# FFT and MLP kernel: when the pieces of w_out are converted in the first tile of tokens

## The chip, the cores and the metric

The program runs on one core of a Trainium2 chip. The metric is the device time of one execution in microseconds (us), as the median of several runs. The times shown come from one chip job, the profile from one more execution of the same program.

## What is computed

The input `x` has 4 batches of 3072 tokens of width 256. Three stages follow each other: the real part of a two-dimensional FFT, a first MLP, and a second, gated MLP.

```python
X = np.fft.fft(np.fft.fft(x, axis=1), axis=2).real      # attention stand-in
h = X @ w_in                                            # 256 -> 2048
y = np.maximum(0.01 * h, h) @ w_out                     # 2048 -> 256
xk = mu_k * y + (1 - mu_k) * y_prev                     # y_prev: one token earlier
xr = mu_r * y + (1 - mu_r) * y_prev
v = np.maximum(xk @ w_k, 0) ** 2 @ w_v
out = v / (1 + np.exp(-(xr @ w_r)))
```

The weights `w_in`, `w_out`, `w_k`, `w_v` and `w_r` arrive as 64-bit floats. [...]

## The kernel before

The whole order of the work is written out by hand, engine by engine; the kernel runs under a manual schedule. Each engine, and each queue of DMA issues (SyncE, called SP, and GpSimd, called POOL), works through its own instructions strictly in order and waits at an instruction until what it needs is there.

The first MLP works on 24 tiles of 512 tokens of the symmetric half, six per batch pair of sums and differences. A tile is a loop over 16 units `u`; unit `u` is one block of 128 of the 2048 hidden columns. `step(x, nx)` (L680) issues one unit's work: on TensorE three matmuls into `ps` for the unit (`mm_b`, L611), three for the next unit (`mm_a`, L599), and then, for the unit **two steps earlier**, the twelve matmuls with `w_out` (`outmm`, L622): four with `gh` and the high part `uoh`, four with `gh` and the low part `uol`, four with `gl` and `uoh`. So unit `u` meets `w_out` in step `u + 2`. On VectorE a step has `g` (L688), `ev` (L604) and `gl` (L670); on ScalarE two leaky-ReLU passes (L108) and `gh` (L105). `mm_b` of a unit waits until `ev` has read `ps`.

In the first tile alone (batch 0, tile 0) the weights of the first MLP are made ready beside this work, by `boot(u)` (L562), which is called after `step` of unit `u`. `w_in` and `w_out` come in eight pieces of 256 rows or columns. Piece `q` of `w_out` serves the units `2q` and `2q + 1`, so its high and low part are first read in step `2q + 2`. The conversion of one piece of `w_out` (built by `f64_hi_lo`, L170) has these instructions:

- `first`: ScalarE `h` (L130) and `st` (L148); VectorE `h` (L134), `fv` (L140) and `h` again (L143); POOL the product `r<-st,h` (L149). Its parts have names: `head` is ScalarE's `h`, then come `one`, `two` and `three` on VectorE, and `tail` is ScalarE's `st` with POOL's product.
- `four`: ScalarE `uoh` (L162) and POOL the sum `r<-r,fv` (L163).
- `five`: VectorE `uol` (L167), the low part, from POOL's sum and `uoh`.

Before the change `boot` calls `first` of piece `q + 1` at the even unit `2q`, `four` at the odd unit after it, and `five` one unit later. The parts of piece 0 are called one by one: `head0()` after the first tile's Q half has been split (L834), `mid0()` (which is `one`, `two` and `three`) and `tail0()` in `boot(0)`.

POOL has other work in the same stretch. From unit 11 of the first tile the rows of the next batch are folded (`fold_ops`, L203): for each of six groups `g`, SP loads two tiles (`first(g)`, L216 and L217), and `second(g)` issues four **accumulating transfers** from POOL's queue (L221 to L224). L221, L223 and L224 all add into the same tile `pm`, so each of them waits on POOL until the one before it has landed. Group 0 is issued in unit 11, group 1 in unit 13, group 2 in unit 16. `next_tab` (L485) issues the load of a DFT table (L199), also from POOL, 1158 KB each; `tab_d` is issued in unit 12. `fft_src` (L281) in unit 11 reads the tile `pm` for the last time (VectorE `t0Qe`, L290) before SP may load the next batch into it.

```python
def second(g):
    E = pm[:, g, 0]
    G.dma_start(E, xs[b, g, :, 1], accum_op=ALU.add)
    G.dma_start(st[g], xs[b, g, :, 2:4], accum_op=ALU.add)
    G.dma_start(E, xs[b, g, :, 2], accum_op=ALU.add)
    G.dma_start(E, xs[b, g, :, 3], accum_op=ALU.add)
```

Of the kernel before, what the change touches and what calls it, by code (L numbers as in the profile page):

```python
# [78 lines left out]
def fft_mlp_kernel(ctx, tc, xs, x7, x8, x87, tb, tbs, alt, ce, so, mu, w_in, w_out, w_k, w_v, w_r, out):  # L79
# [24 lines left out]
    def act_copy(o, i):  # L104
        A.activation(o, i, ACTF.Copy)  # L105
# [4 lines left out]
    def hi_lo(hi, lo, src):  # L110
        act_copy(hi, src)
        V.tensor_tensor(lo, src, hi.bitcast(F32), op=ALU.subtract)  # L112
# [46 lines left out]
    def split_steps(z, k, f, parts):  # L159
        def four():  # L160
            z["p"] = parts()
            A.activation(z["p"][0], z["f"], ACTF.Copy, scale=2.0 ** -8)  # L162
            G.tensor_tensor(z["r"], z["r"], z["f"], op=ALU.add)  # L163

        def five():
            hi, lo = z["p"]
            V.scalar_tensor_tensor(lo, z["r"], 2.0 ** -8, hi.bitcast(F32), op0=ALU.mult, op1=ALU.subtract)  # L167
        return (*f64_steps(z, k, f), four, five)

    def f64_hi_lo(hi, lo, st, k, f, fp, ft):  # L170
        z = {"st": st, "fp": fp, "ft": ft}
        head, one, two, three, tail, four, five = split_steps(z, k, f, lambda: (hi, lo))

        def mid():
            one()
            two()
            three()

        def first():
            head()  # L180
            mid()
            tail()
        return first, four, five, (head, mid, tail)


    TAB = {k: i for i, k in enumerate(["a", "b", "a2", "b2", "c", "d", "c2", "d2"])}
# [109 lines left out]
    def fft_mm(b, kind, h, ps, stop):  # L296
        t = tabs[KINDS[kind][h]]
        how = dict(skip_group_check=True) if h else {}
        if (b, kind[1]) == (0, "o"):
            terms = [(odd0[h][:, c, 0 if kind[0] == "P" else 1], t[:, c]) for c in range(3)]  # L300
        else:
            hi, lo = srcs.pop((b, kind, h))
            terms = [(w[:, c], t[:, i, c]) for c in range(3) for w, i in ((hi, 0), (hi, 1), (lo, 0))]
        fw = FW[kind[1]]
        for n, (w, x) in enumerate(terms):
            T.matmul(ps[:, :fw], w, x[:, :fw], start=(h == 0 and n == 0), stop=(stop and n == len(terms) - 1), **how)  # L306
# [25 lines left out]
    def first_p(ps, ev):  # L332
        fft_mm(0, "Po", 1, ps, True)
        y = pqp.tile([P, CP], F32, tag="P", bufs=2, name="c0Po")
        classes[0, "P", "o"] = y
        hi = mv.tile([P, W], F32R, tag="Ph", bufs=2, name="Ph0_0")
        lo = mv.tile([P, W], F32R, tag="Pl", bufs=2, name="Pl0_0")
        act_copy(hi[:, :J], ps[:, :J])
        V.scalar_tensor_tensor(y[:, J:2 * J], ev[:, :J], 2.0, ps[:, :J], op0=ALU.mult, op1=ALU.subtract)
        V.tensor_tensor(lo[:, :J], ps[:, :J], hi[:, :J].bitcast(F32), op=ALU.subtract)  # L340
        hi_lo(hi[:, J:], lo[:, J:], y[:, J:W])
        return [hi, lo]

    def first_q(ps, ev):
        fft_mm(0, "Qo", 1, ps, True)
        y = pqp.tile([P, CP], F32, tag="Q", bufs=2, name="c0Qo")
        classes[0, "Q", "o"] = y
        act_copy(y[:, :J], ps[:, :J])
        n = W - J
        V.scalar_tensor_tensor(y[:, J:W], ev[:, :n], -2.0, ps[:, :n], op0=ALU.mult, op1=ALU.add)  # L350
        act_copy(y[0:1, :J], cs0[0:1, :J])
        act_copy(y[0:1, J:W], cs0[0:1, J:W])

        def rest():
            V.scalar_tensor_tensor(y[:, W:2 * J], ev[:, n:J], -2.0, ps[:, n:J], op0=ALU.mult, op1=ALU.add)
            act_copy(y[0:1, W:CW["o"]], cs0[0:1, W:CW["o"]])
        return rest
# [9 lines left out]
    def split_tile(b, t, nm):  # L367
        hi = mv.tile([P, W], F32R, tag=nm + "h", bufs=2, name=f"{nm}h{b}_{t}")
        lo = mv.tile([P, W], F32R, tag=nm + "l", bufs=2, name=f"{nm}l{b}_{t}")
        o = 0  # L370
        for par, at, n in PIECES[t]:
            hi_lo(hi[:, o:o + n], lo[:, o:o + n], classes[b, nm, par][:, at:at + n])
            o += n
        return [hi, lo]
# [14 lines left out]
    win, wout, wps = {}, {}, {}  # L389
# [4 lines left out]
    def w_in_load(q, ahead=False):  # L394
        if q < 8:
            win[q] = load_f64(w_in[:, q * 256:(q + 1) * 256].rearrange("(k p) f -> p k f", p=P), 2, 256, ahead)

    def w_in_parts(q):
        if q < 8:
            win[q] = f64_parts(win[q], 2, 256, F32R)  # L400


    def w_in_mm(q, halves=(0, 1)):
        if q >= 8:
            return
        if halves[0] == 0:
            wps[q] = *win[q], ps_s.tile([P, 512], F32, tag="s", name=f"wps{q}")
        fv, r, ps = wps[q]
        win[q] = ps, slice(q * 256, (q + 1) * 256)
        for i in halves:  # L410
            tabl, tabr = ((cet, cer), (sot, sor))[i]
            o = ps[:, i * 256:(i + 1) * 256]
            for k in range(2):
                T.matmul(o, tabl[:, k], fv[:, k], start=(k == 0), stop=False)  # L414
            for k in range(2):
                T.matmul(o, tabr[:, k], r[:, k], start=False, stop=(k == 1))

    def w_in_split(q):
        if q >= 8:
            return  # L420
        ps, sl = win[q]
        o = ps.rearrange("p (i f) -> p i f", i=2)
        act_copy(wh2[:, :, sl], o)
        V.tensor_tensor(wl2[:, :, sl], o, wh2[:, :, sl].bitcast(F32), op=ALU.subtract)


    def w_in_row(q):
        if q >= 8:
            return
        ps = win.pop(q)[0]  # L430
        for i in range(2):
            f = slice((2 * q + i) * P, (2 * q + i + 1) * P)
            o = ps[:, 2 * i:2 + 2 * i]
            T.matmul(o, woh[:, f], one0, start=True, stop=False)
            T.matmul(o, wol[:, f], one0, start=False, stop=True)
        act_copy(w128[:, 2 * q:2 * q + 2], ps[:, 0:4].rearrange("p (i t) -> p i t", t=2)[:, :, 0])

    def w_out_load(q, ahead=False):
        if q < 8:
            st = load_f64(w_out[q * 256:(q + 1) * 256].rearrange("(k p) d -> p k d", p=P), 2, D, ahead)  # L440
            s = slice(2 * q % HF, 2 * q % HF + 2)
            wout[q] = f64_hi_lo(uoh[2 * q // HF][:, s], uol[2 * q // HF][:, s], st, 2, D, *((mv, "gl") if q < 1 else (stage, "f")))
# [107 lines left out]
        fold_odd(g, x0[g])  # L550
    w_in_parts(2)
    cur = first_p(*po)
    rest_q = first_q(*qo)
    head0, mid0, tail0 = wout[0][3]
    rows.release()
    wo = tc.alloc_tile_pool(name="wo", bufs=1)
    wo.tile([P, 80], F32, name="pad2")
# [4 lines left out]
    def boot(u):  # L562
        q = u // 2
        if u == 0:
            w_in_mm(2, (1,))
            mid0()
            tail0()
            wout[0][1]()
            w_in_load(4)
        elif u % 2 == 0:  # L570
            w_in_row(q + 1)
            w_in_mm(q + 2)
            if 1 < q < 8:
                wout[q][2]()
            if q == 1:
                wout[1][1]()
            if q < 7:
                wout[q + 1][0]()
            w_in_load(q + 4)
        else:  # L580
            if q == 0:
                wout[0][2]()
            w_in_split(q + 2)
            if q == 1:
                wout[1][2]()
            if 0 < q < 7:
                wout[q + 1][1]()
            w_in_parts(q + 3)
            if q == 0:
                wout[1][0]()  # L590
            w_out_load(q + 3)

    def mm_a(x):
# [237 lines left out]
    w_in_mm(2, (0,))  # L831
    ev_a(nx)
    cur += split_tile(0, 0, "Q")
    head0()  # L834
    rest_q()
    for b in range(B):

# [3 lines left out]
        for ti in range(NT):  # L841
# [3 lines left out]
            for u in range(NF):  # L845
# [10 lines left out]
                if b == 0 and ti == 0:  # L856
                    boot(u)
# [27 lines left out]
                if i == qe_u + 1:  # L885
                    if b + 1 < B:
                        first, second, fin, _, load7, sum7, fold7 = fold_ops(b + 1)
# [261 lines left out]
```

## Time and profile before

| what | value |
|---|---|
| median of 3 runs | 1490.97 us (1490.51 to 1491.19) |
| profiled execution, own time | 1490.74 us |
| its span, first to last instruction | 1489.0 us |
| TensorE busy | 1472.1 us (99%) |
| VectorE busy | 1032.1 us (69%) |
| ScalarE busy | 893.5 us (60%) |
| POOL busy | 145.2 us (10%) |
| granted TensorE clock | 1.00 over the span |

The profile divides the span into instructions with a start and a length; an idle time in front of an instruction is printed in square brackets with what ended it. DMA-issuing instructions don't count as busy. Matmuls overlap, so the distance between the starts of two of them says more than their printed length. TensorE is busy nearly all the time, so a look at its few idle times tells where the execution can still become shorter, and at which point another engine could make it longer.

### The profile page before, as it was taken

To read this page: it belongs to the slowest core of one execution; us is meant where nothing else is said; L and a number is where in the kernel's file an instruction comes from. 1 tells how busy PE (TensorE), PEld (TensorE's weight loads), DVE (VectorE), ACT (ScalarE), POOL (GpSimd) and SP (SyncE) were. 2 spreads that over 40 slices of the span, in tenths; PEclk is the share of its full clock that TensorE was granted. 3 is DMA by queue.
4 is the path that set the end of the run, shared out by engine and by line. 5 is a ranking of instruction groups with operands and counts; after the bars stand their busy time and mean duration, and the time that the engine had idled before them with its cause. 6 is when DMAs were issued, how large, how long until landed. Compare 5 with 4: busy or idle time off the path is not lost.

```text
span 1489.0 us, 17784 instructions
## 1 busy us (share of the span) xinstructions
PE 1472.1 (99%) x6520; PEld 1210.1 (81%) x6520; DVE 1032.1 (69%) x1444; ACT 893.5 (60%) x1481; POOL 145.2 (10%) x154
## 2 busy tenths in 40 slices
PE   7999999999999999999999999999999999999998
PEld 4687888888888888888888887888888888888887
DVE  7997667666666766666767666676667666666675
ACT  5566566556566565665666666556565655555554
POOL 2444101131010221010000000000000000000000
PEclk9999999999999999999999999999999999999999
DMA  8657223464032654142320102221212112121200
GB/s 311 179 177 161 53 82 125 173 120 91 15 116 92 193 122 69 36 156 66 105 79 0 57 1 98 72 86 45 83 53 76 64 64 67 61 71 57 72 29 29
DMA packets 86396, 134.24 MB, mean 90 GB/s; under 512 B 29283, under 2 KB 49525, under 8 KB 82724
## 3 DMA queue, kind: packets, MB, share of 16 engines
q1 hardware_dynamic: 70916, 86.49, 17.8%
q0 software_dynamic: 15392, 46.61, 12.5%
q8 instruction: 51, 0.84, 0.2%
q14 instruction: 37, 0.30, 0.1%
HBM read 105.20 MB, written 27.88 MB: 89 GB/s over the span
## 4 chain that ended last, share of the span: by engine, by line
PE 95%; DVE 2%; ACT 1%; DMA 0%; issue 0%; POOL 0%; ACTq 0%; DVEq 0%; POOLq 0%
PE o L622 34%; PE v L989 17%; PE kps L946 17%; PE ps L611 9%; PE ps L599 8%; PE rps L997 4%; PE wps L414 1%; DVE fv L140 1%; PE dps L643 1%; PE cps L461 0%; PE f0Po L306 0%; DVE h L134 0%; PE f0Qo L306 0%; DMA st<-in_w_in 0%; DVE g L688 0%
## 5 line engine op out<-in xcount | busy, mean ns | idle before, releaser
L688 DVE SCALAR_TENSOR_TENSOR g<-ev,ps 128x512 f32<-128x512 f32 x192 | 131.8, 686 | 181.6 <-PE ps L611 181.4
L950 ACT ACTIVATE rl<-kps 128x512 f32<-128x512 f32 x190 | 113.5, 597 | 230.7 <-PE kps L946 227.3
L670 DVE TENSOR_TENSOR gl<-g,gh 128x1024 fp32r<-128x1024 f32 x192 | 239.0, 1245 | 1.4 <-ACT gh L105 1.4
L951 DVE SCALAR_TENSOR_TENSOR k<-kps,rl 128x512 f32<-128x512 f32 x190 | 131.4, 692 | 148.6 <-ACT rl L950 147.7
L105 ACT ACTIVATE gh<-g 128x1024 fp32r<-128x1024 f32 x192 | 202.7, 1056 | 49.3 <-PE o L622 47.6
L622 PE MATMUL o<-gh,uol 128*128 128x512 f32 x768 | 211.3, 389 | 1.1 <-DVE uol L167 1.1
L622 PE MATMUL o<-gh,uoh 128*128 128x512 f32 x768 | 211.3, 389 | 0.0
L622 PE MATMUL o<-gl,uoh 128*128 128x512 f32 x768 | 211.1, 389 | 0.0
L108 ACT ACTIVATE g<-ps 128x512 f32<-128x512 f32 x192 | 114.6, 597 | 157.9 <-DVE g L688 156.7
L622 PEld LDWEIGHTS o<-gh,uol 128*128 128x128 f32 x768 | 144.0, 188 | 31.8 <-DVE uol L167 2.0
L622 PEld LDWEIGHTS o<-gh,uoh 128*128 128x128 f32 x768 | 144.2, 188 | 30.5
L622 PEld LDWEIGHTS o<-gl,uoh 128*128 128x128 f32 x768 | 144.2, 188 | 29.9
L604 DVE SCALAR_TENSOR_TENSOR ev<-cb,w,ps 128x512 f32<-128x512 f32 x192 | 143.3, 746 | 2.2 <-PE ps L599 0.4
L112 DVE TENSOR_TENSOR k2l<-k,k2h 128x512 fp32r<-128x512 f32 x190 | 129.6, 682 | 0.5 <-ACT k2h L105 0.5
L989 PE MATMUL v<-k2h,wvh 128*128 128x512 f32 x382 | 121.6, 389 | 0.1
L989 PE MATMUL v<-k2l,wvh 128*128 128x512 f32 x382 | 121.5, 389 | 0.0
L989 PE MATMUL v<-k2h,wvl 128*128 128x512 f32 x382 | 121.5, 389 | 0.0
L108 ACT ACTIVATE g<-g 128x512 f32<-128x512 f32 x192 | 120.0, 625 | 0.0
L946 PE MATMUL kps<-mh,wkh 128*128 128x512 f32 x380 | 117.3, 390 | 1.5 <-ACT mh L105 0.8
L105 ACT ACTIVATE k2h<-k 128x512 fp32r<-128x512 f32 x190 | 118.4, 623 | 0.0
L946 PE MATMUL kps<-ml,wkh 128*128 128x512 f32 x380 | 117.2, 390 | 0.1
L946 PE MATMUL kps<-mh,wkl 128*128 128x512 f32 x380 | 117.1, 389 | 0.0
(409 smaller groups left out, 2254.9 us busy)
## 6 DMA issues: line engine op xcount, KB each, us to landing
y<-yo SPq DMA_DIRECT2D x24, 512.0 KB
xa<-y SPq DMA_DIRECT2D x24, 512.0 KB
out_dram<-o SPq DMA_DIRECT2D x23, 512.0 KB
tab_a<-in_tbs POOLq DMA_DIRECT2D x8, 1158.0 KB, 6.3
tab_b<-in_tbs POOLq DMA_DIRECT2D x8, 1158.0 KB, 5.5
tab_c<-in_tbs POOLq DMA_DIRECT2D x6, 1158.0 KB, 5.6
tab_d<-in_tbs POOLq DMA_DIRECT2D x6, 1158.0 KB, 5.7
pm<-in_xs POOLq DMA_DIRECT2D x54, 128.0 KB, 3.5
```

Of the source, the lines that this page charges most:

```text
L105: A.activation(o, i, ACTF.Copy)
L108: A.activation(o, i, ACTF.Prelu, alpha=0.01)
L112: V.tensor_tensor(lo, src, hi.bitcast(F32), op=ALU.subtract)
L599: T.matmul(x["ps"], l[:, f], r, start=(i == 0), stop=(i == 2))
L604: V.scalar_tensor_tensor(x["ev"], x["cb"], w128[:, u:u + 1], x["ps"], op0=ALU.mult, op1=ALU.add)
L611: T.matmul(x["ps"], l[:, f], r, start=False, stop=(i == 2), skip_group_check=True)
L622: T.matmul(po[s][h], w[:, u % HF, h * P:(h + 1) * P], g[:, s], start=(u == 0 and i == 0), stop=(u == NF - 1 and i == 2))
L670: V.tensor_tensor(gl, x["g"], x["gh"].bitcast(F32), op=ALU.subtract)
L688: V.scalar_tensor_tensor(g[:, 1], x["ev"], 2.0, x["ps"], op0=ALU.mult, op1=ALU.subtract)
L946: T.matmul(ps, w[:, k, sl], x[:, k], start=(i == 0), stop=(i == 5))
L951: V.scalar_tensor_tensor(k2, ps, 0.0, r, op0=ALU.max, op1=ALU.mult)
L989: T.matmul(vps[m], w[:, f, m * P:(m + 1) * P], x, start=(f == 0 and i == 0), stop=(f == NK - 1 and i == 2))
```

## The change

Nothing is added or removed; instructions trade places on VectorE, ScalarE and POOL. TensorE's and SP's orders stay as they are.

- In `boot`, an even unit `2q` (from 2 on) now calls `first` and `four` of piece `q` (not of piece `q + 1`), and the odd unit `2q + 1` calls `five`, between `w_in_split` and `w_in_parts`. The low part of piece `q` is thus made in unit `2q + 1`, just ahead of step `2q + 2`, which reads it.
- The last piece, 7, is started in unit 14 and finished in unit 15, where it was started in unit 12 and finished in unit 13.
- Of piece 0, `head` and `one` run between P's and Q's last steps of the FFT, `two` after Q's split, and `three` and `tail` in `boot(0)`.

```diff
-        def mid():
-            one()
-            two()
-            three()
-
         def first():
-            head()
-            mid()
-            tail()
-        return first, four, five, (head, mid, tail)
+            for g in (head, one, two, three, tail):
+                g()
+        return first, four, five, (head, one, two, three, tail)
...
     cur = first_p(*po)
+    head0, and0, two0, three0, tail0 = wout[0][3]
     rest_q = first_q(*qo)
-    head0, mid0, tail0 = wout[0][3]
+    head0()
+    and0()
...
         if u == 0:
             w_in_mm(2, (1,))
-            mid0()
+            three0()
             tail0()
             wout[0][1]()
             w_in_load(4)
         elif u % 2 == 0:
             w_in_row(q + 1)
             w_in_mm(q + 2)
-            if 1 < q < 8:
-                wout[q][2]()
-            if q == 1:
-                wout[1][1]()
-            if q < 7:
-                wout[q + 1][0]()
+            if q < 8:
+                wout[q][0]()
+                wout[q][1]()
             w_in_load(q + 4)
         else:
-            if q == 0:
-                wout[0][2]()
             w_in_split(q + 2)
-            if q == 1:
-                wout[1][2]()
-            if 0 < q < 7:
-                wout[q + 1][1]()
+            wout[q][2]()
             w_in_parts(q + 3)
-            if q == 0:
-                wout[1][0]()
             w_out_load(q + 3)
...
     cur += split_tile(0, 0, "Q")
-    head0()
+    two0()
     rest_q()
```

POOL, from the fold of group 0 (unit 11) on, before the change. `r<-st,h` and `r<-r,fv` here are product and sum of piece 7; the `pm` and `xl` rows are the accumulating transfers:

```order
L222 DMA xl_0_1013<-in_xs 128x512
L223 DMA pm_1012<-in_xs 128x256
L224 DMA pm_1012<-in_xs 128x256
L149 TENSOR_TENSOR r<-st,h 128x512
L199 DMA tab_d<-in_tbs 128x2316
L163 TENSOR_TENSOR r<-r,fv 128x512
L221 DMA pm_1012<-in_xs 128x256
L222 DMA xl_1_1016<-in_xs 128x512
L223 DMA pm_1012<-in_xs 128x256
L224 DMA pm_1012<-in_xs 128x256
L221 DMA pm_1012<-in_xs 128x256
L222 DMA xl_2_1126<-in_xs 128x512
```

The same place after it:

```order
L216 DMA xl_0_1002<-in_xs 128x512
L217 DMA pm_1001<-in_xs 128x256
L218 DMA pm_1001<-in_xs 128x256
L149 TENSOR_TENSOR r<-st,h 128x512
L163 TENSOR_TENSOR r<-r,fv 128x512
L193 DMA tab_d<-in_tbs 128x2316
L215 DMA pm_1001<-in_xs 128x256
L216 DMA xl_1_1005<-in_xs 128x512
L217 DMA pm_1001<-in_xs 128x256
L218 DMA pm_1001<-in_xs 128x256
L149 TENSOR_TENSOR r<-st,h 128x512
L163 TENSOR_TENSOR r<-r,fv 128x512
```

The first pair is now piece 6's, with the table's load behind both; piece 7's pair stands behind all four transfers of group 1.

VectorE in unit 11, where the tile `pm` is read for the last time, before:

```order
L604 SCALAR_TENSOR_TENSOR ev<-cb_0_245,w_86,ps 128x512
L670 TENSOR_TENSOR gl<-g,gh 128x1024
L424 TENSOR_TENSOR wl_111<-wps_940,wh_110 128x2x256
L290 TENSOR_TENSOR t0Qe_1006<-pm_125 128x384
L112 TENSOR_TENSOR sl0Qe_1008<-t0Qe_1006,sh0Qe_1007 128x384
```

and after:

```order
L590 SCALAR_TENSOR_TENSOR ev<-cb_0_245,w_86,ps 128x512
L656 TENSOR_TENSOR gl<-g,gh 128x1024
L418 TENSOR_TENSOR wl_111<-wps_929,wh_110 128x2x256
L167 SCALAR_TENSOR_TENSOR uol_323<-r,uoh_322 128x512
L284 TENSOR_TENSOR t0Qe_995<-pm_125 128x384
L112 TENSOR_TENSOR sl0Qe_997<-t0Qe_995,sh0Qe_996 128x384
```

The low part of piece 5 now stands ahead of that read.

VectorE at the start of the first tile, before (`ev` is that of units 0, 1 and 2 in turn, `h` and `fv` are of piece 0):

```order
L350 SCALAR_TENSOR_TENSOR c0Qo<-fe0Qo,f0Qo 128x128
L604 SCALAR_TENSOR_TENSOR ev<-cb_0_245,w_86,ps 128x512
L112 TENSOR_TENSOR Ql_0_343<-c0Qo,Qh_0_342 128x512
L355 SCALAR_TENSOR_TENSOR c0Qo<-fe0Qo,f0Qo 128x256
L688 SCALAR_TENSOR_TENSOR g<-ev,ps 128x512
L604 SCALAR_TENSOR_TENSOR ev<-cb_0_245,w_86,ps 128x512
L134 TENSOR_SCALAR h<-h 128x512
L140 SCALAR_TENSOR_TENSOR fv<-st,h 128x512
L143 TENSOR_SCALAR h<-fv 128x512
```

and after:

```order
L344 SCALAR_TENSOR_TENSOR c0Qo<-fe0Qo,f0Qo 128x128
L134 TENSOR_SCALAR h<-h 128x512
L590 SCALAR_TENSOR_TENSOR ev<-cb_0_245,w_86,ps 128x512
L112 TENSOR_TENSOR Ql_0_346<-c0Qo,Qh_0_345 128x512
L140 SCALAR_TENSOR_TENSOR fv<-st,h 128x512
L349 SCALAR_TENSOR_TENSOR c0Qo<-fe0Qo,f0Qo 128x256
L674 SCALAR_TENSOR_TENSOR g<-ev,ps 128x512
L590 SCALAR_TENSOR_TENSOR ev<-cb_0_245,w_86,ps 128x512
L143 TENSOR_SCALAR h<-fv 128x512
```

The first step of piece 0 stands ahead of unit 0's `ev`, the second behind Q's split, the third behind unit 1's `ev`. On ScalarE piece 0's `h` (L130) likewise moves from behind `Qh` to ahead of it.

## Rows read from the trace of the kernel before

**Rows 1.** The page: busy time, share and instructions of each engine.

```profile
PE 1472.1 (99%) x6520; PEld 1210.1 (81%) x6520; DVE 1032.1 (69%) x1444; ACT 893.5 (60%) x1481; POOL 145.2 (10%) x154
```

**Rows 2.** Busy time by stretch (PE, PEld, DVE, ACT, POOL), granted clock, DMA share, GB/s.

```profile
28.00:60.00 32.00, 28.05 (x129) 20.41 (x128) 29.16 (x41) 21.04 (x39) 15.96 (x12) 1.00 0.92 263
60.00:84.00 24.00, 23.42 (x109) 18.69 (x108) 20.71 (x29) 14.38 (x26) 8.48 (x7) 1.00 0.38 127
84.00:130.00 46.00, 46.00 (x218) 38.25 (x217) 41.12 (x61) 31.68 (x57) 21.87 (x21) 1.00 0.59 167
130.00:1489.00 1359.00, 1353.50 (x6001) 1120.28 (x5999) 920.12 (x1264) 815.53 (x1339) 93.24 (x107) 1.00 0.27 78
```

**Rows 3.** TensorE's waits, whole span: us in total, times, longest us.

```profile
PE ps L611 <- DVE ev L604: 2.2, 3, 1.1
PE o L622 <- DVE uol L167: 1.1, 2, 0.7
...
PE wps L414 <- ACT g L108: 0.3, 1, 0.3
```

**Rows 4.** Timeline of PE: start us, length us, what, [idle before <-releaser].

```profile
34.83 0.50 PE L611 MATMUL ps<-Qh,wh 128*128 128x512 f32 x1 [1.14 <-DVE ev L604]
...
38.10 1.20 PE L622 MATMUL o<-gh,uol 128*128 128x512 f32 x4 [0.71 <-DVE uol L167]
```

**Rows 5.** Timeline of ACT and DVE around the first unit.

```profile
28.32 0.75 DVE L604 SCALAR_TENSOR_TENSOR ev<-cb,w,ps 128x512 f32<-128x512 f32 x1 [0.40 <-PE ps L599]
...
28.93 0.66 ACT L130 ACTIVATE h<-st 128x512 f32<-128x512 f32 x1
...
31.92 0.42 DVE L134 TENSOR_SCALAR h<-h 128x512 uint32<-128x512 uint32 x1
```

**Rows 6.** Timeline of POOL, units 11 to 13: fold of groups 0 and 1.

```profile
115.98 0.85 POOL L224 DMA_DIRECT2D pm<-in_xs  x1 [2.73 <-DVE g L688]
116.54 1.63 POOL L149 TENSOR_TENSOR r<-st,h 128x512 f32<-128x512 f32 x1
117.80 0.90 POOL L199 DMA_DIRECT2D tab_d<-in_tbs  x1
118.41 2.01 POOL L163 TENSOR_TENSOR r<-r,fv 128x512 f32<-128x512 f32 x1
120.36 0.85 POOL L221 DMA_DIRECT2D pm<-in_xs  x1
...
125.08 0.85 POOL L223 DMA_DIRECT2D pm<-in_xs  x1 [2.98 <-DMA pm<-in_xs]
128.33 0.85 POOL L224 DMA_DIRECT2D pm<-in_xs  x1 [2.40 <-DMA pm<-in_xs]
```

**Rows 7.** Timeline of DVE, units 11 to 13: piece 7 and the last read of `pm`.

```profile
104.20 1.05 DVE L290 TENSOR_TENSOR t0Qe<-pm 128x384 f32<-128x384 f32 x1
...
110.64 0.48 DVE L143 TENSOR_SCALAR h<-fv 128x512 uint32<-128x512 uint32 x1
...
120.45 0.69 DVE L167 SCALAR_TENSOR_TENSOR uol<-r,uoh 128x512 fp32r<-128x512 f32 x1 [1.19 <-POOL r L163]
```

**Rows 8.** Timeline of PE: low part's matmuls of units 12 and 14.

```profile
116.53 1.07 PE L622 MATMUL o<-gh,uol 128*128 128x512 f32 x4
...
125.80 1.07 PE L622 MATMUL o<-gh,uol 128*128 128x512 f32 x4
```

**Rows 9.** DMA issues, 109 to 130 us: KB each, median us from issue to landing.

```profile
tab_d<-in_tbs POOLq DMA_DIRECT2D x1, 1158.0 KB, 6.0
```

**Rows 10.** Timeline of POOL: a product and a sum with no VectorE work in their way.

```profile
33.78 1.29 POOL L149 TENSOR_TENSOR r<-st,h 128x512 f32<-128x512 f32 x1 [6.43 <-ACT uoh L162]
...
62.84 1.31 POOL L163 TENSOR_TENSOR r<-r,fv 128x512 f32<-128x512 f32 x1
```

**Rows 11.** Timeline of PE: same four matmuls after its first wait, and later.

```profile
6.54 2.07 PE L414 MATMUL wps<-fv,cet 128*128 128x256 f32 x4 [6.54 <-DVE fv L140]
...
11.22 1.15 PE L414 MATMUL wps<-fv,cet 128*128 128x256 f32 x4
```

## Prediction

> **What bounds the kernel now.** The page comes first: TensorE is busy 99% of the span, every other engine 69% or less [rows 1]. So the execution gets shorter only where TensorE stands idle, and any new wait of TensorE lengthens it. The table by stretch says where it stands: between 28 and 84 us it is busy 28.05 of 32 and 23.42 of 24 us, that is 4.5 us idle; from 84 to 130 us it is busy 46.00 of 46.00, and over the other 1359 us it lacks 5.5 [rows 2]. The list of TensorE's waits names the causes in the first stretch: three waits for `ev` (2.2 us), two for a low part `uol` (1.1), one for ScalarE's `g` (0.3) [rows 3]. In that stretch VectorE is busy 29.16 of 32 us [rows 2]; it is the bound there, and what is queued on it early is what TensorE waits for. Past 84 us the reader should see the reverse: TensorE has no idle time left, so a low part that comes late there is a loss in full.
>
> **The change, first part: units 0 to 6.** Two edits work against each other.
>
> Taken away from VectorE's and ScalarE's early queue is one piece's conversion; from unit 1 on one piece fewer has been converted at any moment, and the odd units no longer carry two conversions. I take the waits for `ev` other than the longest as gone (2.2 less the 1.14 at 34.83 us), the second `uol` wait (1.1 less the 0.71 at 38.10 us) and the 0.3 for `g` [rows 3, 4]: 1.1 + 0.4 + 0.3 = 1.8 us. A group of four matmuls that follows a wait takes 1.20 us [rows 4], one that doesn't 1.07 [rows 8], so four waits fewer return another 0.13 each, 0.5 in all. Gain 2.3 us. The wait at 34.83 I leave, since of unit 1's neighbours only one step of piece 0 moves out and one moves in, and the one at 38.10 too, since piece 0's product and sum still follow `three` and `tail` in unit 0.
>
> Added is a delay of the first unit: ScalarE's `h` (0.66) and VectorE's `h` (0.42) of piece 0 now stand ahead of `Qh` and of unit 0's `ev` [rows 5]. Between 0.4 (VectorE's alone) and 1.1 us (both in a row) of that reaches TensorE; `ev` was idle for 0.40 us in front [rows 5], which takes some of the sum, so 0.8.
>
> Net of this part: 2.3 - 0.8 = **1.5 us gained**. Bounds: all of the 4.5 us of idle time goes (3.7 gained), or nothing does (1.1 lost). ScalarE's moved steps cost nothing further, it is idle a third of the time in both stretches [rows 2]; that idle time hides them, and without it `gh` would come later. SP's order stays; the transfers of later pieces wait in their buffers longer, which nobody waits for.
>
> **The change, second part: pieces 6 and 7 behind the fold.** Here the diff's quiet side is. Piece 6 was started in unit 10, ahead of the fold of group 0; now it starts in unit 12, behind it on POOL. Piece 7 moves from unit 12 to unit 14, behind the fold of group 1. POOL waits at L223 and at L224 until the transfer before has landed, and everything queued behind waits along. The trace shows that this is no fine point: piece 7's product had its last input from VectorE at 110.64 + 0.48 = 111.1 us [rows 7] and started only at 116.54, 0.56 us behind L224 [rows 6]. It did no harm, because unit 14's low part was not read before 125.80 us [rows 8] and was made at 120.45 [rows 7]. Now piece 6 takes that very place, and it is due when unit 12 meets it, at 116.53 us [rows 8].
>
> All times below are on the old clock; the fold starts from `t0Qe` of unit 11, which VectorE reaches earlier by the gain of the first part, so that gain shifts everything alike and is subtracted at the end.
>
> - *Start.* Piece 5's `uol` (0.69) now stands ahead of `t0Qe` [rows 7], which must end before SP may reload `pm`. `t0Qe` took 1.05 us beside POOL's sum there and could be shorter; between 0 and 0.7, I take 0.3. The product of piece 6 starts at 116.54 + 0.3 = 116.8.
> - *Piece 6.* Product and sum take 1.29 and 1.31 us with nothing in their way [rows 10], and VectorE sits waiting, so nothing is; with 0.1 between them POOL is done at 119.5. `uol` takes 0.69 more: 120.2, where 116.53 was wanted. **TensorE waits 3.7 us in step 14.**
> - *Table.* `tab_d` was issued at 117.80 between product and sum [rows 6]; now behind both, at 119.5. It lands 6.0 us after issue [rows 9]: 125.5 where it was 123.8.
> - *Group 1.* Its first transfer, L221, was issued at 120.36 and the next that needs it at 125.08 [rows 6], 4.7 us later, where L223 to L224 is 3.25 (125.08 to 128.33). I read that as L221 standing behind the table in POOL's one queue: L223 came 1.3 us after the table's landing. So L223 now goes at 126.8, L224 at 130.0.
> - *Piece 7.* Product 0.56 us behind L224, at 130.6; with the sum done at 133.3; `uol` at 134.0. Due 125.80 [rows 8]: **8.2 us late**, of which 3.7 are already spent in step 14. With 0.13 for the restart, 8.3.
>
> Behind that `uol` VectorE has `g` and `ev` of the next unit to do (0.75 for `ev` [rows 5]), while TensorE still has eight matmuls with `w_out`; no further wait follows. The fold's later groups come later by as much, and what they make is read in unit 37, over twenty units on, so that costs nothing.
>
> Bounds: if product and sum are stretched as in the old trace (1.63 and 2.01, [rows 6]), each pair takes 1.0 more: 10.3 late. If the table does not hold up group 1, L221 goes at 120.1, L223 at 123.4, L224 at 126.6, `uol` is there at 130.6: 4.9 late.
>
> **Sum.** 8.3 - 1.5 = 6.8 us on top of the profiled execution's own 1490.74: 1497.5 us. The median of the runs lies 0.23 above that execution, so I forecast **1497.8 us**, 0.46% slower.
>
> **Rivals.**
>
> *The low parts are there in time.* The price is the first part alone: 1491.0 - 1.5 = 1489.5, at the best bound 1487.3. The place is POOL between 104 and 117 us: it decides if the way from `t0Qe` to piece 6's `uol` is 3.7 us shorter than I work out, and that to piece 7's 8.2 us. Against it stands the old trace, in which POOL's product waited out the transfers for 5.4 us with its inputs ready [rows 6, 7]; for it only that the new order's transfers are in no row yet. Chance 0.08, a quarter of it below 1488.0.
>
> *The table is not in the way.* Then 4.9 - 1.5 = 3.4: 1494.4. For it speaks that I infer the queueing from a single 4.7 against 3.25. Chance 0.15.
>
> *TensorE comes back slowly from a pause.* After its 6.54 us of waiting at the start the same four matmuls took 2.07 us, and from 11.22 us on 1.15 [rows 11]: twice the time, as at 1.2 in place of 2.4 GHz, although the granted clock is printed as 1.00 in all stretches shown [rows 2]. The slow stretch runs from 6.54 to 11.22, 4.7 us, of which half is lost: 2.3. The pauses of the forecast are 3.7 us in step 14 and 8.2 - 3.7 = 4.5 in step 16; a slow return from the first is swallowed by the second, whose end POOL sets, so one such loss counts: 1500.1. The longest pause after the start was 1.14 us [rows 4], so the trace can't tell what 4 us do. Chance 0.2. The Trainium skill (TensorE: Matmul & The Clock Gate, "Part 1: The HAM clock gate") says that half rate is the state after an idle spell and that only sustained work lifts it; by that rule the sum would be 1500.1, without it 1497.8. The trace agrees with it at the start, and no row here shows it later.
>
> **How the numbers follow.** The forecast has 0.57, with its own range of 1495.5 to 1499.8. To hold 8 in 10 the range goes from **1494.2** (just under the case without the table) to **1501.0** (the slow return, or stretched pairs with little gained early). A measurement of this kernel tells about 0.2% from no change, 3 us. Slower by more than that, above 1494.0: forecast, slow return and two thirds of the table's case, 0.87. Within it: the rest of that case and most of the first rival, 0.11. Faster: 0.02.
>
> **What the changed profile would show.** Two new waits of TensorE, `o L622` for `uol L167`, of some 4 and 4.5 us, in the place where the old table has 46.00 of 46.00; VectorE's two `uol` there idle behind POOL's sum; piece 7's sum on POOL near 132 us; TensorE some 1 to 2 us ahead of the old trace at unit 10. If those two waits are missing, or under 2 us each, the second part is wrong; if the waits for `ev` and the second `uol` still stand before 60 us, the first is. If matmuls behind the long waits run at double their length, the slow return holds.

## The result, and the profile after

The changed kernel takes 1501.7 us (median of 6 runs, 1500.45 to 1502.34), the kernel before, run beside it, 1490.91 (6 runs). The ratio is 1.0071, 95% interval 1.0058 to 1.0084: 10.8 us slower, where 6.8 were forecast. The range ended at 1501.0 and did not hold the time. The sign and the place were right, the size 4 us short. The profiled execution took 1500.71 us, span 1498.9; its span is 9.9 us longer than that of the profile before (1489.0), and its own time lies 1.0 below the median of its runs. The sums below explain the 9.9.

The table by stretch, in the columns of [rows 2]:

```profile
28.00:60.00 32.00, 29.78 (x141) 22.46 (x140) 25.04 (x39) 20.30 (x37) 16.69 (x13) 1.00 0.89 259
60.00:84.00 24.00, 24.00 (x118) 20.13 (x117) 22.49 (x34) 16.34 (x29) 7.27 (x6) 1.00 0.36 116
84.00:130.00 46.00, 40.97 (x177) 32.94 (x175) 32.34 (x51) 27.68 (x49) 18.64 (x17) 0.93 0.60 166
130.00:1498.90 1368.90, 1359.58 (x6019) 1124.56 (x6018) 924.57 (x1270) 818.31 (x1343) 97.14 (x110) 1.00 0.27 78
```

The first two stretches gained, as they were meant to: VectorE is busy 25.04 us where it was 29.16, and TensorE has no idle time left from 60 to 84 us. The third lost 5.0 us of TensorE, and its granted clock is 0.93 on the mean. TensorE's waits (us in total, times, longest), which answer to [rows 3]:

```profile
PE o L608 <- DVE uol L167: 9.5, 3, 5.0
...
PE ps L597 <- DVE ev L590: 1.7, 2, 0.8
```

The waits for `uol` grew from 1.1 to 9.5 us (of each piece of the 64-bit `w_out` the kernel makes two single-precision tensors, the high part `uoh` and the low part `uol`). Where the waits stand shows TensorE's timeline, which answers to [rows 8] (start, length, what, idle before and its releaser); the rows with `Qh,wh` are the first matmuls of units 14 and 17:

```profile
110.27 0.50 PE L597 MATMUL ps<-Qh,wh 128*128 128x512 f32 x1
...
111.76 1.09 PE L608 MATMUL o<-gh,uoh 128*128 128x512 f32 x4
117.89 2.08 PE L608 MATMUL o<-gh,uol 128*128 128x512 f32 x4 [5.03 <-DVE uol L167]
...
124.43 1.09 PE L608 MATMUL o<-gh,uoh 128*128 128x512 f32 x4
...
129.04 1.07 PE L608 MATMUL o<-gh,uoh 128*128 128x512 f32 x4
134.00 2.00 PE L608 MATMUL o<-gh,uol 128*128 128x512 f32 x4 [3.89 <-DVE uol L167]
...
137.98 0.40 PE L597 MATMUL ps<-Qh,wh 128*128 128x512 f32 x1
```

The same two first matmuls in the kernel before:

```profile
114.26 0.39 PE L611 MATMUL ps<-Qh,wh 128*128 128x512 f32 x1
...
128.08 0.39 PE L611 MATMUL ps<-Qh,wh 128*128 128x512 f32 x1
```

So TensorE reaches unit 14 earlier by 114.26 - 110.27 = 4.0 us, and unit 17 later by 137.98 - 128.08 = 9.9. In between lie four losses, 13.9 us together. The four matmuls with `uol` would have started 0.91 us behind the 111.76 and the 129.04 (the distance of such groups in an unhindered step); they start 5.2 and 4.1 us late. And after each wait TensorE runs slowly for a while: from 117.89 to the next step's group with `uoh`, 124.43, are 6.54 us, where the same work took 3.67 in the kernel before (116.53 to 120.20); from 134.00 to unit 17 are 3.98 us, where it took 2.28 (125.80 to 128.08). That is 2.9 and 1.7 us, and 5.2 + 4.1 + 2.9 + 1.7 = 13.9. The table by stretch gives the granted clock (the third column from the right):

```profile
120.00:122.00 2.00, 2.00 (x6) 1.10 (x6) 1.93 (x4) 1.34 (x3) 0.00 (x0) 0.50 0.98 320
...
124.00:126.00 2.00, 2.00 (x10) 1.64 (x9) 1.90 (x4) 1.82 (x3) 0.00 (x0) 1.00 0.88 154
...
134.00:136.00 2.00, 2.00 (x5) 1.62 (x6) 1.89 (x3) 1.11 (x2) 0.91 (x2) 0.53 0.52 76
...
138.00:140.00 2.00, 2.00 (x10) 1.65 (x9) 1.01 (x2) 1.77 (x3) 0.00 (x0) 1.00 0.85 178
```

It is 0.50, the lower of the two levels, or close to it (0.53, where a stretch holds a little of both) for some time behind each wait, and 1.00 in the stretches from 84 to 116 us, ahead of the first wait, and again from 124 and from 138 us.

POOL's timeline answers to [rows 6]:

```profile
113.60 0.85 POOL L218 DMA_DIRECT2D pm<-in_xs  x1 [2.40 <-DMA pm<-in_xs]
114.16 1.60 POOL L149 TENSOR_TENSOR r<-st,h 128x512 f32<-128x512 f32 x1
115.85 1.26 POOL L163 TENSOR_TENSOR r<-r,fv 128x512 f32<-128x512 f32 x1
117.05 0.59 POOL L193 DMA_DIRECT2D tab_d<-in_tbs  x1
117.64 0.89 POOL L215 DMA_DIRECT2D pm<-in_xs  x1
...
126.45 0.86 POOL L217 DMA_DIRECT2D pm<-in_xs  x1 [7.04 <-DMA pm<-in_xs]
129.71 0.86 POOL L218 DMA_DIRECT2D pm<-in_xs  x1 [2.40 <-DMA pm<-in_xs]
130.27 1.61 POOL L149 TENSOR_TENSOR r<-st,h 128x512 f32<-128x512 f32 x1
131.96 1.26 POOL L163 TENSOR_TENSOR r<-r,fv 128x512 f32<-128x512 f32 x1
```

and VectorE's to [rows 7]:

```profile
101.39 0.55 DVE L284 TENSOR_TENSOR t0Qe<-pm 128x384 f32<-128x384 f32 x1
...
117.14 0.69 DVE L167 SCALAR_TENSOR_TENSOR uol<-r,uoh 128x512 fp32r<-128x512 f32 x1 [5.80 <-POOL r L163]
...
133.25 0.69 DVE L167 SCALAR_TENSOR_TENSOR uol<-r,uoh 128x512 fp32r<-128x512 f32 x1 [6.43 <-POOL r L163]
```

Piece 6's product and sum (114.16, 115.85) stand behind L218 of group 0, piece 7's (130.27, 131.96) behind L218 of group 1, and VectorE sits idle for 5.80 and 6.43 us until POOL's sum lets it make `uol`. Between them POOL waits 7.04 us for the transfer that L215 issued, right behind `tab_d`.

### The profile page after: what moved, and what is told of

Read it like the earlier page. It is cut to its first block, busy times and chain, and to the rows that moved or that the text cites. A ratio compares the mean times of both kernels' runs of the same rounds, so it can differ in the third digit from the quotient of the medians.

```text
span 1498.9 us, 17784 instructions
## 1 busy us (share of the span) xinstructions
PE 1475.7 (98%) x6520; PEld 1212.7 (81%) x6520; DVE 1025.5 (68%) x1444; ACT 893.8 (60%) x1481; POOL 145.4 (10%) x154
## 4 chain that ended last, share of the span: by engine, by line
PE 90%; DVE 1%; DMA 1%; POOL 1%; issue 0%; ACT 0%; POOLq 0%; ACTq 0%; DVEq 0%
PE o L608 32%; PE v L975 17%; PE kps L932 17%; PE ps L597 8%; PE ps L585 8%; PE rps L983 4%; DMA pm<-in_xs 1%; PE dps L629 0%; POOL r L163 0%; POOL r L149 0%; PE f1Qe L300 0%; PE f2Qe L300 0%; DMA y<-yo 0%; PE f3Qe L300 0%; PE f3Pe L300 0%
```

## The experiments

All times are medians, with the ratio to the kernel before (1490.8 to 1490.9 in each comparison) and its interval. Diffs are against the changed kernel, except where another is named. "Unit 17" is the start of that unit's first matmul with `Qh,wh`.

### Which part: the spread of piece 0, or pieces 6 and 7

`late_only` puts piece 0's steps back where they were:

```diff
     rest_q = first_q(*qo)
-    head0()
-    and0()
...
             w_in_mm(2, (1,))
+            and0()
+            two0()
             three0()
...
-    two0()
+    head0()
     rest_q()
```

> The changed kernel with piece 0's steps back where they were (all of its VectorE steps in unit 0). Theory (the early gain comes from the pieces moved later; the spread of piece 0's steps only costs 0.8 us at the first unit): TensorE's 0.8 us wait ahead of its first Q matmul goes, units 3 to 12 are as early as in the changed kernel or up to 0.8 us earlier, and since POOL's fold sets the end of both waits the total stays within 1 us of the changed kernel's 1501.7. Rival (the spread brings part of the gain): unit 14 starts 1 to 2 us later than in the changed kernel (111 to 112 us), the total is 1502 to 1503.

1500.99 us, ratio 1.0069 (1.0054 to 1.0084). Unit 14 comes at 110.30 and unit 17 at 138.52: early gain and late loss are both there. The wait of 0.81 us in front of the first unit, which the spread of piece 0 costs, is gone here, but two later waits are longer (1.12 for 0.84 us, 0.71 for 0.53), and unit 3 starts at 42.87 where the changed kernel has 42.86. In the total the spread is worth less than this comparison can tell.

`early67` leaves the change to pieces 0 to 5. It starts piece 6 in unit 11, on POOL ahead of the fold of group 0, and piece 7 in unit 12, behind group 0 but ahead of the table and of group 1:

```diff
-            if q < 8:
+            if q < 6:
                 wout[q][0]()
                 wout[q][1]()
+            if q == 6:
+                wout[6][2]()
+                wout[7][0]()
+                wout[7][1]()
             w_in_load(q + 4)
...
-            wout[q][2]()
+            if q != 6:
+                wout[q][2]()
+            if q == 5:
+                wout[6][0]()
+                wout[6][1]()
             w_in_parts(q + 3)
```

> The changed kernel, but pieces 6 and 7 keep places ahead of or right at the first fold group: piece 6 is started in unit 11 ahead of the fold of group 0 on POOL, and piece 7 in unit 12, ahead of the table. Theory (the loss is the two sums that queue behind accumulating transfers, and the slow clock that these waits bring): both waits of TensorE for a low part after 84 us go, no stretch runs at a granted clock below 1.00, and the early gain of 4.0 us that the changed kernel shows at unit 14 (110.27 against 114.26 us) stays to the end: about 1487.0 us, 1486.3 to 1488.3. Rival (the early gain is only borrowed, later waits take it back whatever the place of pieces 6 and 7): 1490 to 1491.

1491.01 us, ratio 0.9998 (0.9989 to 1.0008). No wait for `uol` is left in units 12 to 16, so 10.7 us of loss hang on the place of these two pieces. But the early gain is gone too, and the time is the rival's. TensorE's timeline and the granted clock of one stretch show where:

```profile
113.32 0.50 PE L605 MATMUL ps<-Qh,wh 128*128 128x512 f32 x1 [1.97 <-DVE ev L598]
...
114.90 1.91 PE L616 MATMUL o<-gh,uoh 128*128 128x512 f32 x4
...
118.23 1.09 PE L616 MATMUL o<-gl,uoh 128*128 128x512 f32 x4
```

```profile
116.00:118.00 2.00, 2.00 (x6) 1.52 (x6) 1.20 (x2) 0.56 (x2) 1.91 (x2) 0.50 0.51 136
```

One new wait for `ev`, 1.97 us, and behind it a stretch at 0.50, in which the same four matmuls take 1.91 us in place of 1.07. Ahead of that `ev` VectorE had waited 0.57 us for ScalarE's `c0Qe`, which ran at 110.28, behind piece 7's `uoh` at 109.74. So the gain was spent at one new place; `early67b` to `early67e` below get part of it back, which speaks against the rival's reason.

### The tables in POOL's queue

`table_later` issues `tab_d` in unit 20; `tabs_later` issues `tab_c` there and `tab_d` in unit 22 (both are read from unit 37 on):

```diff
-                    if i in (k_u, k_u + lag):
+                    if i in (k_u, k_u + lag) and i != 12 or b == 0 and i == 20 and kind == "Qe":
                         next_tab()
```

```diff
-                    if i in (k_u, k_u + lag):
+                    if i in (k_u, k_u + lag) and i not in (10, 12) or b == 0 and i in (20, 22) and kind == "Qe":
                         next_tab()
```

> The changed kernel with the load of table d issued in unit 20 instead of 12. Theory (the first transfer of fold group 1 stands behind the table in POOL's queue): that transfer lands 3 us after its issue and not 8.3 us, piece 7's low part is ready near 127.5 us, before TensorE asks for it at 130; the second wait and its slow stretch go, the first wait (5 us and 2.9 us of slow clock) stays. Sum: 1490.9 - 4.0 + 5.2 + 2.9 = 1495.0 us, 1494.3 to 1496. Rival (the transfers are slow for another reason, such as the loads of SP beside them): the second wait stays, 1500 to 1502.

> The changed kernel with both tables issued later, tab_c in unit 20 and tab_d in unit 22, so that neither stands in POOL's queue near the fold. With tab_d alone moved the time was 1497.4. Theory (tab_c holds up the fold's group 0 as tab_d does group 1: in every trace so far group 0's first transfer is issued 0.4 to 1.6 us behind the landing of tab_c, however early SP's load before it was issued): that first transfer comes about 1.8 us earlier, the wait in step 14 shrinks from 5 or 6 to 3 or 4 us, and the time is 1495.0 to 1496.0. Rival (SP's own loads take that long, table or not): no change against the run with tab_d alone, 1497.0 to 1497.7.

1497.35 us (ratio 1.0043, 1.0028 to 1.0058) and 1494.56 (1.0024, 1.0014 to 1.0034): 4.3 us less than the changed kernel with one table out of the way, 7.1 with both. The first came out 2.4 us above what was expected: its second wait fell to 0.58 us, but the first was 6.4. The second came in below its range. TensorE's timeline of `tabs_later`:

```profile
117.00 2.07 PE L608 MATMUL o<-gh,uol 128*128 128x512 f32 x4 [3.89 <-DVE uol L167]
118.87 1.91 PE L608 MATMUL o<-gl,uoh 128*128 128x512 f32 x4
...
129.25 0.97 PE L608 MATMUL o<-gh,uol 128*128 128x512 f32 x3 [0.26 <-DVE uol L167]
```

and POOL's:

```profile
104.83 0.90 POOL L215 DMA_DIRECT2D pm<-in_xs  x1 [3.85 <-DVE ev L590]
...
108.22 0.85 POOL L217 DMA_DIRECT2D pm<-in_xs  x1 [1.58 <-DMA pm<-in_xs]
112.71 0.85 POOL L218 DMA_DIRECT2D pm<-in_xs  x1 [3.65 <-DMA pm<-in_xs]
...
116.16 0.87 POOL L215 DMA_DIRECT2D pm<-in_xs  x1
...
119.39 0.90 POOL L217 DMA_DIRECT2D pm<-in_xs  x1 [1.47 <-DMA pm<-in_xs]
...
128.42 0.85 POOL L215 DMA_DIRECT2D pm<-in_xs  x1
```

Group 1's first transfer is issued at 116.16 and the next at 119.39, 3.2 us later; with `tab_d` ahead of it this took 126.45 - 117.64 = 8.8. And `tab_c` had held group 0: SP's load of `pm`, on another queue, is issued at 102.19 and POOL's first transfer on top of it at 104.83, 2.6 us, where the changed kernel has 101.96 and 107.07, 5.1 us. Behind the 3.89 us wait the matmuls still run at half rate, and without the second such wait only one slow stretch is left.

### The fold itself

`fold_later` leaves both pieces and both tables where the change has them, starts the fold's transfers on POOL in unit 16, and closes the first group in unit 18 in place of 13:

```diff
-        pe_u, qe_u, f0, f1 = (5, 10, 13, 36) if b == 0 else (1, 4, 10, 36)
+        pe_u, qe_u, f0, f1 = (5, 10, 18, 36) if b == 0 else (1, 4, 10, 36)
...
                         load7()
-                        second(0)
+                if b + 1 < B and i == (16 if b == 0 else qe_u + 1):
+                    second(0)
```

> The changed kernel with the fold's first transfers on POOL moved from unit 11 to unit 16, and the first group's closing from unit 13 to unit 18; pieces 6 and 7 stay where the change put them. Theory (only the fold's transfers ahead of them in POOL's queue make pieces 6 and 7 late): both long waits for uol go, with them the slow stretches of the clock, and the 4.0 us gained before unit 14 stay: 1490.9 - 4.0 = 1486.9, between 1486.0 and 1488.5. Rival (piece 6, begun in unit 12, is late by its own steps even with POOL free): a wait of 1 to 3 us stays in step 14, a slow stretch behind it, and the time is 1489 to 1492. Second rival (the later fold collides with what reads it in unit 37): above 1492 with a new wait after unit 30.

1490.15 us, ratio 0.9994 (0.9985 to 1.0003), 11.5 us less than the changed kernel. Both waits for `uol` in units 12 to 16 are gone, as the theory says; the time lies in the first rival's range all the same, but not for its reason. Two waits for `ev` came, 1.75 us at 112.08 and 1.03 at 122.56, with no slow stretch behind either. VectorE's timeline ahead of the first:

```profile
107.76 1.25 DVE L322 SCALAR_TENSOR_TENSOR c0Qe<-fe0Qe,c0Qe 128x384 f32<-128x384 f32 x1 [0.62 <-ACT c0Qe L105]
108.93 1.51 DVE L112 TENSOR_TENSOR Pl<-c0Po,Ph 128x256 fp32r<-128x256 f32 x1
110.36 0.41 DVE L112 TENSOR_TENSOR Pl<-c0Pe,Ph 128x256 fp32r<-128x256 f32 x1
```

`c0Qe` took 0.54 us in the kernel before and a `Pl` 0.41; here they take 1.25 and 1.51 while POOL's product and sum of piece 6 run (107.28 to 110.15), and the second `Pl`, which starts behind that sum, 0.41 again.

### The half clock behind a wait

`fill` puts matmuls that nobody reads between the groups with `uoh` and with `uol`, 20 in unit 12's and 28 in unit 14's; `fill2` has 31 and 18.

```diff
+            if n == 4 and fills:
+                dps = ps_s.tile([P, 512], F32, tag="s", name="fill")
+                for _ in range(fills):
+                    T.matmul(dps, wh[:, u % HF, :P], gh[:, 0], start=True, stop=True)
...
+        fills = {12: 20, 14: 28}.get(x["u"], 0) if (x["b"], x["t"]) == (0, 0) else 0
```

> The changed kernel with matmuls put into TensorE's two waits: 20 in step 14 and 28 in step 16, between the group with the high part and the group with the low part, into a spare accumulator that nobody reads. They add work that the product does not need. Theory (TensorE's clock falls to half because it stands idle in the waits): the low parts are ready when they were, the groups behind take 1.07 and not 2.0 us, the granted clock stays 1.00; 2.9 us less behind the first wait, which only lengthens the second wait, and 1.7 us less behind the second: 1500.0 us against 1501.7, and the spread between runs shrinks. Rival (the slow groups come from something else, such as late operands): they stay at 2 us and the time at 1501 to 1502.

> The changed kernel with matmuls that nobody reads in the two pauses, 31 in step 14 and 18 in step 16 (the run before had 20 and 28: the 20 ended 2.5 us before uol came and the clock still fell, the 28 ran 2.3 us past uol). Theory (the half clock behind the second pause costs 1.7 us of the end, that behind the first costs nothing since the second pause takes it in): no slow stretch, and 1.3 to 1.9 us less than the changed kernel, 1499.8 to 1500.4. Rival (the slow stretch costs nothing at the end, because VectorE or POOL is behind anyway): 1501.2 to 1502.

`fill`: 1501.47 us, ratio 1.0071 (1.0056 to 1.0086), nothing gained. Behind the 20 TensorE still stood idle for 2.53 us, and the granted clock was 0.50 from 122 to 124 us all the same; the 28 ran 2.3 us past the end of `uol` (137.39 against 135.05), which cost more than the clock, 1.00 there, gave back. `fill2`: 1500.35 us, ratio 1.0063 (1.0048 to 1.0078). Here the clock stays at 1.00 throughout, and the last pause is 1.06 us:

```profile
130.34 4.24 PE L610 MATMUL fill<-gh,uoh 128*128 128x512 f32 x18
135.64 1.20 PE L612 MATMUL o<-gh,uol 128*128 128x512 f32 x4 [1.06 <-DVE uol L167]
136.68 1.08 PE L612 MATMUL o<-gl,uoh 128*128 128x512 f32 x4
...
138.06 0.40 PE L597 MATMUL ps<-Qh,wh 128*128 128x512 f32 x1
```

From 135.64 to unit 17 are 2.42 us, in place of the 3.98 of the changed kernel: 1.6 us of the second slow stretch come back. In the total 1.35 us show, and the two intervals overlap. Nor does this execution reach unit 17 earlier (138.06 for 137.98): POOL's chain was slower in it, and `uol` of piece 7 was there at 135.58 for 133.94. So the trace shows that without idle time the clock stays at 1.00 and what the slow stretch takes locally; that the end comes earlier by as much is likely and not shown. That the first slow stretch costs nothing is argued: POOL sets the end of the second wait, whatever TensorE did before.

### A version that beats both

`early67b` is `early67` with piece 7's `four` (ScalarE's `uoh` and POOL's sum) in unit 13; `early67c` moves its `first` (`h`, `fv`, `h`, the product) there too; `early67d` takes `four` on to unit 14; `early67e` is `early67c` with both tables late, as in `tabs_later`. The core of `early67c` against `early67`:

```diff
             if q == 6:
                 wout[6][2]()
-                wout[7][0]()
-                wout[7][1]()
...
+            if q == 6:
+                wout[7][0]()
+                wout[7][1]()
             w_in_parts(q + 3)
```

> As the run before with pieces 6 and 7 early, but ScalarE's uoh of piece 7 (the step called four) goes from unit 12 to unit 13, where the kernel before had it. That run came out at 1491.0 in place of 1487.0; its trace shows one wait of 1.97 us for ev at 111.35 us, with uoh of piece 7 ahead of c0Qe in ScalarE's queue, and 3.4 us of half clock behind the pause. Theory (uoh held c0Qe, c0Qe held Pl and ev, and the pause cost 1.97 + 1.7): the wait goes and the clock stays at 1.00: 1487.0 to 1487.8. Rival (VectorE has too much to do in unit 12 whatever the order): the wait is still over 1 us, and the time 1489.5 to 1491.5.

1488.95 us, ratio 0.9987 (0.9978 to 0.9996). The wait for `ev` shrank to 1.28 us, no stretch at half clock follows, and 2.1 us against `early67` are won (the two intervals overlap a little); 1 us above the theory, below the rival.

> As the run with uoh of piece 7 in unit 13, but all of piece 7's first steps go to unit 13 too (h, fv, h and uoh there). In that run a wait for ev of 1.28 us was left at 112.36 us, with h, fv, h of piece 7 (1.5 us on VectorE) ahead of c0Qe, Pl and ev. Theory (those 1.5 us make the wait, and POOL can't begin piece 7's product before the fold's third transfer of group 0 anyway): the wait goes, nothing new comes, 1487.2 to 1488.2. Rival (ScalarE, in order, now waits for VectorE's fv in front of gh of unit 13, or h, fv, h hold up the next ev): a new wait of 1 us or more in units 14 or 15, 1488.7 to 1490.

1488.99 us, ratio 0.9987 (0.9978 to 0.9996): the rival's time. The wait of 1.28 us went, and one of 1.03 came at 121.49, from another cause than the rival named:

```profile
116.86 1.61 DVE L112 TENSOR_TENSOR Ql<-c0Qo,Qh 128x256 fp32r<-128x256 f32 x1 [0.17 <-ACT Qh L105]
118.39 1.51 DVE L112 TENSOR_TENSOR Ql<-c0Qe,Qh 128x256 fp32r<-128x256 f32 x1
```

Two `Ql` take 1.61 and 1.51 us beside POOL's product and sum of piece 7 (116.53 to 119.62), 0.42 elsewhere.

> As early67c, but uoh of piece 7 goes on to unit 14, so that ScalarE has no step there that waits for VectorE's fv in front of gh of unit 13. Theory: like early67c where that one gains, 1487.2 to 1488.2, and faster than it where ScalarE holds it up. Rival (uol of piece 7 comes late, since POOL's sum now follows later): a wait for uol in step 16, 1489 or more.

1498.28 us, ratio 1.0049 (1.0036 to 1.0063). With `four` in unit 14, POOL's sum falls behind group 1's transfers, and the old case is back in one place, a wait of 8.02 us with half rate behind it:

```profile
115.54 1.64 POOL L149 TENSOR_TENSOR r<-st,h 128x512 f32<-128x512 f32 x1
116.81 1.20 POOL L215 DMA_DIRECT2D pm<-in_xs  x1
...
124.86 0.86 POOL L217 DMA_DIRECT2D pm<-in_xs  x1 [5.96 <-DMA pm<-in_xs]
...
128.74 1.59 POOL L163 TENSOR_TENSOR r<-r,fv 128x512 f32<-128x512 f32 x1
```

The sum stands in POOL's queue behind group 1's transfers, and the first of these (116.81) behind the table, issued at 114.97.

> As early67c, with both tables issued in units 20 and 22 as well. In early67c the wait of 1.28 us for ev went, and one of 1.03 us came at 121.49 us: VectorE's two Ql took 1.61 and 1.51 us there (0.41 elsewhere) beside POOL's product and sum of piece 7 (116.53 to 119.62 us). Theory (POOL's work beside them stretches the Ql, and the tables hold up the fold's transfers ahead of that product): without the tables product and sum end 2 to 3 us earlier, the Ql take about 0.4 us again, the wait goes, and the time is 1487.3 to 1488.3. Rival (the product still falls on Ql, or stretches what VectorE does before): a wait for ev of about 1 us stays, 1488.7 to 1489.5.

1488.07 us, ratio 0.9983 (0.9974 to 0.9992), within the theory's range: the lowest median here, 2.9 us under the kernel before and 13.6 under the changed one. Its interval overlaps those of `early67b` and `early67c`, so that it beats these two is not shown. POOL's sum ends at 118.39, so one `Ql` is still slowed and one is not, and the wait for `ev` is 0.50 us:

```profile
117.15 1.52 DVE L112 TENSOR_TENSOR Ql<-c0Qo,Qh 128x256 fp32r<-128x256 f32 x1
118.59 0.41 DVE L112 TENSOR_TENSOR Ql<-c0Qe,Qh 128x256 fp32r<-128x256 f32 x1
```

## Why the prediction was wrong, step by step

**The mechanism held.** Two waits of TensorE for `uol`, behind a fold that POOL's queue puts in front: `fold_later` takes the fold away from in front of the two pieces, `early67` puts piece 6 ahead of group 0 and piece 7 ahead of group 1, and both waits go; `tabs_later` takes the tables away and two thirds of the loss go. That POOL's product and sum take their 1.3 us each with VectorE waiting was nearly right (1.60 and 1.26), though VectorE was not out of the way in [rows 10]: `gl` ran beside the end of the product there, and `t0Pe` beside the sum.

**The early gain was 4.0 us, not 1.5, and outside the forecast's bound of 3.7.** The wait in front of the first unit was sized rightly (0.81 us, 0.8 forecast), but it does not belong in the net gain: by `late_only` it is made up by unit 3. The waits given back were mis-sized. The prediction listed those before 60 us; two more, 0.25 us at 65.18 and 0.34 at 79.41 before, went too, and the 23.42 of 24.00 in [rows 2] had shown them. The wait at 34.83, which was left in place, shrank from 1.14 to 0.84. And a wait costs more than is printed in front of it: the overlap with the matmul before is lost as well. At 44.03 us 0.73 was printed; from the matmuls before it, 42.72, to it are 1.31 us where the changed kernel has 0.42 (42.44 to 42.86), so 0.89 went with the wait, and 0.11 more until the next matmul: 0.27 above what is printed, where the forecast put 0.13.

**"That gain shifts everything alike" was wrong.** A gain on TensorE in front of a wait that another engine ends is waited away; only what reaches POOL's chain counts. Of the 4.0 us VectorE's read of `pm` got 3.3 (`t0Qe` ends at 101.94 for 105.25), POOL's first transfer of group 0 got 2.0 (107.07 for 109.03), as SP's load under it took longer beside `tab_c` (5.1 us until that transfer, 3.8 before, 2.6 without the table), and piece 6's product 2.4 (114.16 for 116.54). Piece 6 was thus ready at 117.83, 0.9 us earlier than worked out. This error does not make the miss, since by itself it makes the time shorter; and that a gain put too low and a shift put too high came out so near each other was luck. With the true 4.0 shifted alike the working gives 8.3 - 4.0 = 4.3 us slower.

**What failed in the sum, first: the step "Group 1", where the 1.3 us between the table's landing and the next transfer of the chain (L223 before, L217 now) were 3.0.** `tab_d` lands 6.4 us after its issue, at 123.45; L217 follows at 126.45. The prediction took 1.3 from one case of the kernel before, in which POOL's sum stood between `tab_d` and the first transfer of group 1; now that transfer follows the table by 0.59 us. From there the working nearly holds: L218 after 3.26 us (3.25 forecast), the product 0.56 behind it as forecast, the end of `uol` 3.7 behind the start of the product (3.4 forecast). It is there at 133.94, where the forecast's own steps with its 1.5 us give 132.5: 1.4 us, with the 0.9 won at piece 6 already taken off.

**What failed in the sum, second: the slow return was left out of it.** It stood among the rivals, with a chance of 0.20. Its working was right, one loss that counts and one that the second wait takes in; it measured 1.7 us, 2.3 were put down. So 6.8 + 1.4 + 1.7 = 9.9, the difference of the spans. The rest of the distance to the median, 1501.7, is that the profiled execution was one of the changed kernel's faster ones. The chance was too low: TensorE's slow start stood in [rows 11], and after it no row had a wait over 1.14 us that spoke against. The start was a hint only: from 6 to 12 us the trace prints a granted clock of 1.00, so there it is the length of the matmuls alone that agrees with a half rate, and whether the start and the stretches behind the waits have one cause is not shown.

The Trainium skill (TensorE: Matmul & The Clock Gate, "Part 1: The HAM clock gate") has the half rate as the state after idling, lifted by sustained work. The trace of the changed kernel agrees: 0.50 behind the waits of 5.03 and 3.89 us, and 1.00 again from 124 and from 138 us, TensorE having worked on without a pause.

Two things stay open. How SP's load and group 1's first transfer came to take 5.1 and 8.8 us beside a table was not followed packet by packet; that the tables do it is shown only by taking them away. And the first wait of `table_later`, 6.4 us, 1.4 longer than the changed kernel's, is explained in part only: unit 14 comes 0.9 us later there (111.21), but POOL's first transfer of group 0 1.5 us later (108.59), and from L217 to L218 are 3.77 us for 3.25. Why these take longer is open.

## What to carry to other kernels

A step that is moved "later, but still in time" must be checked on the in-order queue of every engine that it passes through; here two small steps on POOL fell behind transfers whose landing POOL waits for, and behind a table load that nobody needed for another twenty units. A gain ahead of a wait that another engine ends is not a gain, so follow it along that engine's chain before adding it. Where TensorE is the bound, price a pause of some microseconds at its length plus the slow matmuls behind it, and look for long transfers that can be issued after the crowded place instead of in it.

## What the runs showed of the hardware

**VectorE beside POOL.** An operation of VectorE on two SBUF tensors took nearly four times as long while a tensor operation of POOL ran: `Ql` 1.51 to 1.61 us in place of 0.42, `Pl` 1.51 for 0.41. The Trainium skill (SBUF — State Buffer, "SBUF: two separate sides") says that the two share a port pair which one instruction holds to its end, also where VectorE's operation has two SBUF inputs and POOL's reads SBUF. The rows agree: the slowed one ends 0.3 to 0.4 us behind POOL's operation, and one that runs behind POOL's last takes 0.41. In `fold_later` and `early67c` waits of TensorE of 1.0 to 1.75 us follow such operations; that these cause them is argued from the order, and `early67e`, where one `Ql` was fast again, has 0.50.

**A table load slows the transfers beside it.** From SP's load of `pm` to POOL's transfer on top of it were 2.6 us without `tab_c` in flight and 5.1 with it, though the table is on POOL's queue. From the transfer behind `tab_d` on POOL's own queue to the one that waits for it were 3.2 and 8.8.

**Which pauses were followed by half clock.** In these traces the granted clock was 0.50 behind TensorE's pauses of 1.97 us (`early67`), 2.53 (`fill`) and all longer ones but the one at the start (1.00 behind it), and stayed at 1.00 behind those of 1.28 (`early67b`) and 1.75 us (`fold_later`). Each of these is one execution. Of the ten runs of `early67` five have a mean granted clock of 0.999 and five of 1.000, so its half-clock stretch is probably not in every run, and no bound follows from the list.
